# A gated convolution with expert routing: where the second part's routing and the first part's scatters stand

## Chip, cores, metric

The kernel runs on one core of a Trainium2 chip. The metric is the device time of one execution in microseconds (us), as the median of several. All data is float32. The core's engines are TensorE (PE; its weight loads are shown as PEld), VectorE (DVE), ScalarE (ACT), GpSimd (POOL) and SyncE (SP), which here only issues transfers. Each engine runs its instructions in the order of the program and waits on semaphores for the others.

## What is computed

Eight sequences of 3584 tokens with 192 channels pass a causal convolution with 7 softmax-weighted taps per head, and then a layer of 8 experts in which a token may take over the expert of the token before it.

```python
# lightweight convolution: w = softmax(weight) over the 7 taps of each of 8 heads
out[b, s, h] = sum_k w[h, k] * x_pad[b, s + k, h]          # then x = out

logits     = x @ w_gate                                    # (B, S, 8)
local_gate = sigmoid(x @ w_local)
for b in range(B):
    prev_e = -1
    for s in range(S):
        fresh_e = argmax(logits[b, s])
        e = fresh_e if s == 0 or local_gate[b, s] < 0.5 else prev_e
        prev_e = e
        p = softmax(logits[b, s])
        h = maximum(x[b, s] @ w1[e], 0)                    # 192 -> 1024
        out[b, s] = p[e] * (h @ w2[e])                     # 1024 -> 192
```

## The kernel before

The 28672 tokens are worked through in 16 parts of 1792 tokens. For each part the kernel convolves, routes (which expert, which slot among that expert's tokens) and scatters the rows to `slots` in memory, sorted by expert, by indirect transfers of GpSimd. Blocks of 128 tokens (the first 35) and then of 256 tokens of one expert each are loaded from there, multiplied with that expert's weights, and their results are scattered to the output. Tables say which block is which expert's. Blocks 0 to 6 need rows of part 0 only, 7 to 13 rows of part 0 and the first half of part 1, 14 to 20 parts 0 and 1.

Parts 0 and 1 are convolved on TensorE (`wide`) and routed by `wide_route`. Blocks 0 and 1 do not wait for the scatters: their rows are picked by matrix products with one-hot matrices (`hots`, `gather`, `gathered`).

```python
def wide_route(g, y_sb, lt):                  # a generator; the caller takes it on stage by stage
    ...                                       # VectorE: fr, fc, mx, ex
    yield                                     # 1
    ...                                       # VectorE: eq, key
    nc.scalar.activation(ex, ex, Act.Exp)     # L419
    ...                                       # VectorE: fc (L420)
    yield                                     # 2
    ...                                       # TensorE: two transposes of fc (L426)
    yield                                     # 3
    mark["nf", g] = nc.vector.tensor_copy(nf, rps[:, 1, :])
    ...                                       # VectorE: scans; run (L452)
    nc.tensor.transpose(bps, run, identity=ident[:NB, :NB])          # L454
    ...
    yield                                     # 4
    mark["oh", g] = nc.vector.tensor_tensor(oh, bcast_mid(bps, E), bcast(en[:TB], NB),
                                            op=Alu.is_equal)
    ...                                       # TensorE: counts of oh (L468, L469)
    yield                                     # 5
    mark["upto", g] = nc.vector.tensor_tensor_scan(...)
    ...                                       # VectorE: slots of the tokens
    for b in range(NB):                       # 16 scatters stand ready
        to_put.append((HALF if g and b < NH else g, y[:, b, :], posi[:, b:b + 1]))
    yield                                     # 6
    if g == 0:
        first_table(upto[:, :, NB], pos)      # which has hots(0) in its middle
    ...
    if g:
        for _ in tables(g):                   # small VectorE instructions
            pass

def hots(i):                                  # 4 VectorE instructions (L550)
    ...
def gather(i, y_sb, ps, blocks):
    for b in blocks:
        nc.tensor.matmul(ps[:, :Y0 + D], lhsT=hot[:TB, i, b, :], rhs=y_sb[:TB, b, :Y0 + D],
                         start=(b == 0), stop=(b == NB - 1))         # L556
def gathered(ps):
    xg = xp.tile([P, KT, DG], F32, name="xg")
    nc.scalar.copy(xg[:, 0, :Y0 + D], ps[:, :Y0 + D])                # L561
    ...
    return xg
```

`put` sends one scatter from GpSimd, behind another instruction if one is named. The convolution of part 2 and later parts is done by VectorE and ScalarE (`conv`), and `step(t)` takes it, or a later part's routing, on by about t us of VectorE's time.

```python
def conv(g, x_sb):
    ...
    def first(h):                             # ScalarE (L378)
        nc.scalar.activation(cols(h), chans(h, 0), Act.Copy, scale=c[:, h, 0:1])
    first(0)
    yield 0
    for h in range(H):
        if h + 1 < H:
            first(h + 1)
        ...
        for k in range(1, KC):                # VectorE (L388)
            nc.vector.scalar_tensor_tensor(cols(h), chans(h, k), c[:, h, k:k + 1],
                                           cols(h), Alu.mult, Alu.add)
            yield 0.6
```

A block is `turn` (its rows transposed on TensorE), `hidden` (first product, relu on ScalarE) and `output` (second product). `output` writes the two `yps` buffers, which ScalarE and then VectorE read. The start of the block phase:

```python
puts_behind(None, 5)                          # 5 scatters of part 0
rest(route0)                                  # the first table
some(wide1, WIDE - 20)
...
weights(AHEAD - 1)                            # weights of three blocks
picks = [yps_p.tile([P, 512], F32, name="yps")]
gather(0, ya, picks[0], range(4))
rest(wide1)
puts_behind(mark["lt", 1], 3)
route1 = wide_route(1, yb, got.pop(1))
some(route1, 2)
hots(1)
gather(0, ya, picks[0], range(4, NB))
next(route1)
xgs[0] = gathered(picks[0])
...                                           # gather(1), turn of block 0, gathered(1) among
...                                           # the stages of route1 and two steps (1.8, 2.4)
puts_behind(mark["upto", 1], 4)
rest(route1)
for i, (_, n, _, _) in enumerate(blocks):
    ensure(i)                                 # row loads up to three blocks ahead
    weights(i + AHEAD)
    ...
    hT = hidden(n, wbs[i], xT, (1, 1) if i else (0, 0))     # (1, 1): scatters behind its relus
    if i + 1 < len(blocks):
        xT, copied = turn(blocks[i + 1][1], xgs[i + 1])
        ...
    step(2.1 if n == 1 else 4.2)
    output(n, wbs.pop(i), xgs.pop(i), hT)                   # has a step(1.2) inside
    step(1.3 if n == 1 else 3.0)
```

Of the kernel before, what the change touches and what calls it, by code (L numbers as in the profile page):

```python
# [17 lines left out]
P = 128  # L18
# [11 lines left out]
NB = 16  # L30
# [40 lines left out]
def bcast(ap, n):  # L71

    return ap.rearrange("p (a o) -> p a o", o=1).to_broadcast([ap.shape[0], ap.shape[1], n])


def bcast_mid(ap, n):

    return ap.rearrange("p (o a) -> p o a", o=1).to_broadcast([ap.shape[0], n, ap.shape[1]])
# [3 lines left out]
def kernel(  # L82
# [100 lines left out]
        nc.vector.tensor_copy(c.rearrange("p h k -> p (h k)"), cps[:, H:H + H * KC])  # L183
    wgb, wgq = wg[:, :3, :], wg[:, 3:, :]

    got, mark = {}, {}

# [5 lines left out]
    def wide(g, xv, y_sb, both):  # L195

        lps = yps_p.tile([P, 512], F32, name="yps")[:, :4 * TB].rearrange("p (q s) -> p q s", s=TB)  # L200
        count = [0]

        def mine():
            count[0] += 1
            return both and count[0] % 2 == 0

        def convolve(half, heads):
            bs = slice(half * NH, (half + 1) * NH)
            for h in heads:
                ps = hps_p.tile([P, 512], F32, name="hps")[:TB, :NH * GS]  # L210
                nc.tensor.matmul(ps, lhsT=hank[:NI, h, :],
                                 rhs=xv[:NI, bs, h * GS:(h + 1) * GS], start=True, stop=True)
                to = y_sb[:TB, bs, Y0 + h * GS:Y0 + (h + 1) * GS]
                at = ps.rearrange("p (b d) -> p b d", d=GS)
                if mine():
                    nc.vector.tensor_scalar(to, at, rz[:TB, h:h + 1], None, Alu.mult)
                else:
                    nc.scalar.activation(to, at, Act.Copy, scale=rz[:TB, h:h + 1])
                yield

        def again(half):
            bs = slice(half * NH, (half + 1) * NH)
            nc.gpsimd.tensor_copy(yr[:, bs, :], y_sb[:TB, bs, Y0 + P:Y0 + D])
            nc.gpsimd.tensor_copy(y_sb[:TB, bs, Y0 + D:IX], y_sb[:TB, bs, Y0:Y0 + DR])

        def turned(half, qs):
            at = half * 3 * NH // 2
            for q in qs:
                tps = hps_p.tile([P, 512], F32, name="hps")[:, :4 * TB].rearrange(
                    "p (u s) -> p u s", s=TB)  # L230
                for u in range(4):
                    b = half * NH + (q * 4 + u if q < 2 else 2 * u)
                    src = (y_sb[:TB, b, Y0:Y0 + P] if q < 2
                           else yr[:, b:b + 2, :].rearrange("p b d -> p (b d)"))
                    nc.tensor.transpose(tps[:, u, :], src, identity=ident[:TB, :TB])
                leave = nc.vector.tensor_copy if mine() else nc.scalar.copy
                leave(yT[:, at + 4 * q:at + 4 * q + 4, :], tps)
                yield

        def products():  # L240
            for j in range(4):
                u = j // 2 * 3 * NH // 2 + j % 2 * 4
                nc.tensor.matmul(lps[Q * j:Q * j + Q], lhsT=wgb[:, 0, :], rhs=yT[:, u:u + 4, :],
                                 start=True, stop=False, skip_group_check=True)
            for i in range(2):
                for j in range(4):
                    u = j // 2 * 3 * NH // 2 + NH + j % 2 * 2
                    nc.tensor.matmul(lps[Q * j:Q * j + Q, i::2, :], lhsT=wgb[:, 1 + i, :],
                                     rhs=yT[:, u:u + 2, :], start=False, stop=(i == 1),
                                     skip_group_check=True)  # L250

        yield from convolve(0, range(H))
        zy = z_tile()
        yT = zy[:, :3 * NH * TB].rearrange("p (u s) -> p u s", s=TB)
        yr = zy[:TB, 3 * NH * TB:].rearrange("p (b d) -> p b d", d=DR)
        again(0)
        yield from convolve(1, range(5))
        yield from turned(0, (0, 1))
        yield from convolve(1, range(5, H))
        yield from turned(0, (2,))  # L260
        again(1)
        yield from turned(1, range(3))
        products()
        if both:
            nc.vector.tensor_copy(lsb[:, :2, :], lps[:, :2, :])
            nc.scalar.copy(lsb[:, 2:, :], lps[:, 2:, :])
        else:
            nc.scalar.copy(lsb, lps)
        yield
        ltp = yps_p.tile([P, 512], F32, name="yps")[:TB].rearrange("p (q c) -> p q c", c=P)  # L270
        for q in range(4):
            nc.tensor.transpose(ltp[:, q, :], lsb[:, q, :], identity=ident)
        lt = sm.tile([P, NB, E + 1], F32, name="lt")[:TB]
        mark["lt", g] = nc.vector.tensor_copy(lt.rearrange("p (j q) e -> p j q e", q=4),
                              ltp.rearrange("p q (j c) -> p j q c", c=Q)[:, :, :, :E + 1])
        got[g] = lt

# [116 lines left out]
    def wide_route(g, y_sb, lt):  # L394
# [41 lines left out]
        yield  # L436
        run = sm.tile([NB, TB], F32, name="run")
        nf = sm.tile([NB, TB], F32, name="nf")
        mark["nf", g] = nc.vector.tensor_copy(nf, rps[:, 1, :])
        nc.vector.tensor_tensor_scan(run, nf, rps[:, 0, :], 0.0, Alu.mult, Alu.add)  # L440

        nc.vector.tensor_reduce(rows[:NB, 1, 0:1], nf, axis=AX.X, op=Alu.min)
# [17 lines left out]
        if g:  # L460
            norm()
        yield
        oh = sm.tile([P, E, NB], F32, name="oh", bufs=1)[:TB]
        mark["oh", g] = nc.vector.tensor_tensor(oh, bcast_mid(bps, E), bcast(en[:TB], NB),
                                                op=Alu.is_equal)


# [5 lines left out]
        nc.vector.tensor_reduce(pr, eq, axis=AX.X, op=Alu.add)  # L473
        yield
        upto = sm.tile([P, E, 1 + NB], F32, name="upto")
        mark["upto", g] = nc.vector.tensor_tensor_scan(upto.rearrange("p e b -> p (e b)"),
                                     go_on.rearrange("p e b -> p (e b)"),
                                     nps[:, :E * (1 + NB)], 0.0, Alu.mult, Alu.add)
        at = sm.tile([P, E, NB], F32, name="at", bufs=1)[:TB]
# [23 lines left out]
    def first_table(upto, pos):  # L503
# [24 lines left out]
        nc.vector.scalar_tensor_tensor(rel, bcast(r2[:TB], NB), -float(UT), bcast_mid(pos, 2),  # L528
                                       Alu.mult, Alu.add)
        rels.append(rel)  # L530
        hots(0)

        inn = sm.tile([P, E], F32, name="inn")
        nc.vector.tensor_scalar(inn, end[:, :E], i_of, None, Alu.is_le)
# [12 lines left out]
    def hots(i):  # L547
        for b in range(0, NB, NB // 4):
            bs = slice(b, b + NB // 4)
            nc.vector.tensor_tensor(hot[:TB, i, bs, :], bcast(rels[0][:, i, bs], UT),  # L550
                                    bcast_mid(slot[:TB], NB // 4), op=Alu.is_equal)
# [218 lines left out]
    def put(behind=None):  # L770


        if not to_put:
            return
        g, rows, to = to_put.pop(0)
        nc.gpsimd.nop()
        ins = nc.gpsimd.indirect_dma_start(  # L777
            out=slots[:, :], in_=rows, in_offset=None,
            out_offset=bass.IndirectOffsetOnAxis(ap=to, axis=0)).ins
        if behind is not None:  # L780
            tc.add_manual_dep(ins, behind.ins.name, SYNC, reason="scatters apart")
        if puts:
            tc.declare_no_dep(ins, group="puts", reason="slots of their own")
        if g:
            tc.declare_no_dep(ins, group="gets", reason="those slots were full before")
        puts.append((g, ins))
        tc.add_to_no_dep_group("puts", ins)
        tc.add_to_no_dep_group(f"puts{g}", ins)
# [285 lines left out]
    for n in (4, 3, 5, 1, 3, 0):  # L1074
        next(route0)
        some(wide1, n)

    def puts_behind(ins, n):
        for _ in range(n):
            put(ins)  # L1080

    puts_behind(None, 5)
    rest(route0)
    some(wide1, WIDE - 20)

# [23 lines left out]
    weights(AHEAD - 1)  # L1109


    picks = [yps_p.tile([P, 512], F32, name="yps")]
    gather(0, ya, picks[0], range(4))
    rest(wide1)
    puts_behind(mark["lt", 1], 3)
    route1 = wide_route(1, yb, got.pop(1))
    some(route1, 2)
    hots(1)
    gather(0, ya, picks[0], range(4, NB))
    next(route1)  # L1120
    xgs[0] = gathered(picks[0])
    picks.append(yps_p.tile([P, 512], F32, name="yps"))
    gather(1, ya, picks[1], range(9))
    next(route1)
    puts_behind(mark["nf", 1], 2)
    step(1.8)
    xT, _ = turn(blocks[0][1], xgs[0])
    gather(1, ya, picks[1], range(9, NB))
    next(route1)
    puts_behind(mark["oh", 1], 2)  # L1130
    step(2.4)
    xgs[1] = gathered(picks[1])
    next(route1)
    puts_behind(mark["upto", 1], 4)
    rest(route1)
    for i, (_, n, _, _) in enumerate(blocks):
        st["block"] = i
        ensure(i)
        weights(i + AHEAD)
        if i == LATE:  # L1140
            x_in[3] = load_x(3)
        hT = hidden(n, wbs[i], xT, (1, 1) if i else (0, 0))
        if i + 1 < len(blocks):
            xT, copied = turn(blocks[i + 1][1], xgs[i + 1])
            if len(to_put) > NT // 2 and n == KT:
                put(copied)
        step(2.1 if n == 1 else 4.2)
        output(n, wbs.pop(i), xgs.pop(i), hT)
        step(1.3 if n == 1 else 3.0)

    kind, _, at, group = spare[0]
# [78 lines left out]
```

## Time and profile before

| | us |
|---|---|
| time, median of 3 | 1355.3 (1355.29 to 1356.96) |
| span of the profiled execution | 1351.2 |
| TensorE busy | 1327.7 |
| VectorE busy | 780.0 |
| ScalarE busy | 512.1 |
| GpSimd busy | 492.6 |

A line of the timeline gives the start in us from the span's start, the duration in us, the engine, the kernel's line, the operation with the tiles it writes and reads and their sizes, how many instructions are merged into the line, and in brackets how long the engine stood idle before it and what ended the wait. A line of the windows gives, for a stretch of time, its length, the busy time of each engine with the count of instructions in the order PE, PEld, DVE, ACT, POOL, and at the end the share of the TensorE clock that was granted, the busy share of the DMA engines, and GB/s. A line of the waits gives who waited for whom, the sum in us, the number of times, and the longest. Starts of matmuls are recorded; their ends are modelled.

### The profile page before, as it was taken

To read this page: it belongs to the slowest core of one execution; us is meant where nothing else is said; L and a number is where in the kernel's file an instruction comes from. 1 tells how busy PE (TensorE), PEld (TensorE's weight loads), DVE (VectorE), ACT (ScalarE), POOL (GpSimd) and SP (SyncE) were. 2 spreads that over 40 slices of the span, in tenths; PEclk is the share of its full clock that TensorE was granted. 3 is DMA by queue.
4 is the path that set the end of the run, shared out by engine and by line. 5 is a ranking of instruction groups with operands and counts; after the bars stand their busy time and mean duration, and the time that the engine had idled before them with its cause. 6 is when DMAs were issued, how large, how long until landed. Compare 5 with 4: busy or idle time off the path is not lost. (4 is left out here: it accounts for less than half of the span.)

```text
span 1351.2 us, 41902 instructions
## 1 busy us (share of the span) xinstructions
PE 1327.7 (98%) x17140; PEld 1298.5 (96%) x17140; DVE 780.0 (58%) x2434; ACT 512.1 (38%) x1147; POOL 492.6 (36%) x538
## 2 busy tenths in 40 slices
PE   8899999999999999999999999999999999999998
PEld 7799999999999999999999999999999999999997
DVE  6878887886868787868787878786610000000000
ACT  5244443433343433333334343433333333333333
POOL 4455343534243434343434343434344211221111
PEclk9899999999999999999999999999999999999999
DMA  5899999967575757575757575756566555556993
GB/s 185 291 343 402 365 364 337 389 245 268 199 272 195 289 195 291 198 273 203 280 202 287 196 287 198 289 203 228 199 232 228 199 183 182 190 189 232 322 325 124
DMA packets 67299, 340.39 MB, mean 252 GB/s; under 512 B 12576, under 2 KB 23191, under 8 KB 47650
## 3 DMA queue, kind: packets, MB, share of 16 engines
q1 hardware_dynamic: 44784, 284.88, 58.7%
q0 software_dynamic: 22320, 52.82, 10.3%
q8 instruction: 136, 2.23, 0.6%
q14 instruction: 57, 0.47, 0.1%
q10 hardware_dynamic: 2, 0.00, 0.0%
HBM read 284.73 MB, written 53.41 MB: 250 GB/s over the span
## 5 line engine op out<-in xcount | busy, mean ns | idle before, releaser
L977 PE MATMUL yps<-wb,hT 64*128 64x192 f32 x7328 | 652.9, 326 | 9.6 <-ACT hT L965 7.7
L960 PE MATMUL hps<-xT,wb 64*128 64x256 f32 (+1 forms) x6816 | 640.2, 337 | 0.6 <-issue 0.6
L977 PEld LDWEIGHTS yps<-wb,hT 64*128 64x128 f32 x7328 | 609.7, 188 | 21.0 <-ACT hT L965 14.0
L960 PEld LDWEIGHTS hps<-xT,wb 64*128 64x128 f32 x6816 | 610.0, 188 | 8.4 <-issue 1.8
L993 POOL DMA_INDIRECT out_dram<-o_sb,xg x229 | 232.4, 1015 | 613.7 <-DVE o_sb L989 545.9
L965 ACT ACTIVATE hT<-hps 128x512 f32<-128x512 f32 (+1 forms) x568 | 262.3, 512 | 407.5 <-PE hps L960 306.8
L388 DVE SCALAR_TENSOR_TENSOR y_sb<-x_sb,c,y_sb 128x336 f32<-128x336 f32 x672 | 377.0, 571 | 19.5 <-ACT y_sb L378 1.4
L989 DVE SCALAR_TENSOR_TENSOR o_sb<-yps,xg,o_sb 128x192 f32<-128x192 f32 x229 | 87.4, 413 | 489.1 <-ACT o_sb L985 474.5
L777 POOL DMA_INDIRECT slots<-y_sb,posi x228 | 227.7, 999 | 216.0 <-ACT hT L965 112.0
L985 ACT ACTIVATE o_sb<-yps,xg 128x192 f32<-128x192 f32 x229 | 86.9, 418 | 379.1 <-PE yps L977 368.7
L946 ACT COPY xT<-xps 128x768 f32<-128x768 f32 (+1 forms) x142 | 96.7, 681 | 5.3 <-issue 1.6
L360 PEld LDWEIGHTS xps<-ident,xg 64*128 64x128 f32 x1374 | 81.9, 139 | 2.7
L360 PE MATMUL xps<-ident,xg 64*128 64x64 f32 x1374 | 80.4, 222 | 0.0
L378 ACT ACTIVATE y_sb<-x_sb,c 128x336 f32<-128x336 f32 x112 | 64.6, 589 | 0.0
L572 DVE STREAM_TRANSPOSE z<-y_sb 128x768 f32<-128x768 f32 (+1 forms) x56 | 45.4, 852 | 0.4
L598 DVE COPY lt<-lq 32x36 f32<-32x36 f32 x224 | 41.0, 183 | 3.5
L582 PE MATMUL hps<-z,wg 64*32 64x128 f32 x1344 | 24.1, 272 | 0.7 <-issue 0.6
L582 PEld LDWEIGHTS hps<-z,wg 64*32 64x32 f32 x1344 | 19.1, 105 | 3.4 <-issue 2.6
L556 PE MATMUL yps<-y_sb 112*128 112x194 f32 x64 | 12.5, 351 | 1.8 <-DVE y_sb L550 1.6
L556 PEld LDWEIGHTS yps<-y_sb 112*128 112x128 f32 x64 | 11.2, 201 | 2.6 <-DVE y_sb L550 2.0
L590 DVE STREAM_TRANSPOSE lq<-ls 128x256 f32<-128x256 f32 x14 | 6.2, 444 | 12.4 <-ACT ls L587 12.4
L568 POOL COPY y_sb<-y_sb 128x896 f32<-128x896 f32 x14 | 13.4, 954 | 0.0
(239 smaller groups left out, 374.4 us busy)
## 6 DMA issues: line engine op xcount, KB each, us to landing
wb<-in_w_dram SPq DMA_DIRECT2D x138, 1536.0 KB
x_sb<-in_x_dram SPq DMA_DIRECT2D x14, 1920.0 KB
xg<-slots SPq DMA_DIRECT2D x87, 259.0 KB
xg<-slots SPq DMA_DIRECT2D x53, 129.5 KB
wb<-in_w_dram SPq DMA_DIRECT2D x12, 512.0 KB
out_dram<-o_sb,xg POOLq DMA_INDIRECT x229
slots<-y_sb,posi POOLq DMA_INDIRECT x228
x_sb<-in_xb_dram SPq DMA_DIRECT2D x4, 768.0 KB
```

The lines of the kernel that those rows point to most:

```text
L360: nc.tensor.transpose(to, src[rows], identity=ident[rows, rows])
L378: nc.scalar.activation(cols(h), chans(h, 0), Act.Copy, scale=c[:, h, 0:1])
L388: nc.vector.scalar_tensor_tensor(cols(h), chans(h, k), c[:, h, k:k + 1], cols(h), Alu.mult, Alu.add)
L572: nc.vector.transpose(z[:, t:u, :], y_sb[:, t:u, Y0:Y0 + D])
L777: ins = nc.gpsimd.indirect_dma_start(out=slots[:, :], in_=rows, in_offset=None, out_offset=bass.IndirectOffsetOnAxis(ap=to, axis=0)).ins
L946: copied = nc.scalar.copy(to, at)
L960: nc.tensor.matmul(hps[half][:, j, w], lhsT=wb[rows, f0:f0 + P], rhs=xT[rows, d, w], start=(d == 0 and j == 0), stop=(d == KD - 1), skip_g ...
L965: relu = nc.scalar.activation(hT[:, m:m + 2, w], hps[half][:, :, w], Act.Relu)
L977: nc.tensor.matmul(yps[half][:, k * D:(k + 1) * D], lhsT=hT[rows, m, k * P:(k + 1) * P], rhs=wb[rows, WA + m * D:WA + (m + 1) * D], start= ...
L985: nc.scalar.activation(o_sb[:, k, :], y[k][0], Act.Copy, scale=xg[:, k, 0:1])
L989: nc.vector.scalar_tensor_tensor(o_sb[:, k, :], y[k][1], xg[:, k, 0:1], o_sb[:, k, :], Alu.mult, Alu.add)
L993: sent = nc.gpsimd.indirect_dma_start(out=out, in_=o_sb[:, k, :], in_offset=None, out_offset=bass.IndirectOffsetOnAxis(ap=xg.bitcast(I32)[ ...
```

## The change

Part 0's 16 scatters, which stood in groups of 5, 3, 2, 2 and 4 behind marked VectorE instructions, are issued in one row. The one-hot matrices of block 0 are made after the first table and no longer in its middle. Both gathers are done in one loop with nothing of part 1's routing in it, and the step of the convolution follows them in one piece. The routing of part 1 is then spread: two stages ahead of the blocks, one in block 0, two in block 1, and the rest ahead of block 2; since its scatters are ready later, blocks 2 and 3 send three each and not two. Fewer waits are tied to marked instructions this way, and block 0 no longer has the whole routing of part 1 ahead of it. The results are the same.

```diff
@@ first_table
         rels.append(rel)
-        hots(0)
 
         inn = sm.tile([P, E], F32, name="inn")
@@ before the blocks
-    puts_behind(None, 5)
+    while to_put:
+        put()
     rest(route0)
     some(wide1, WIDE - 20)
...
-    picks = [yps_p.tile([P, 512], F32, name="yps")]
-    gather(0, ya, picks[0], range(4))
+    for i in range(2):
+        hots(i)
+        pick = yps_p.tile([P, 512], F32, name="yps")
+        gather(i, ya, pick, range(NB // 2))
+        if i:
+            xT, _ = turn(blocks[0][1], xgs[0])
+        gather(i, ya, pick, range(NB // 2, NB))
+        xgs[i] = gathered(pick)
+    step(5.4)
     rest(wide1)
-    puts_behind(mark["lt", 1], 3)
     route1 = wide_route(1, yb, got.pop(1))
     some(route1, 2)
-    hots(1)
-    gather(0, ya, picks[0], range(4, NB))
-    next(route1)
-    xgs[0] = gathered(picks[0])
-    picks.append(yps_p.tile([P, 512], F32, name="yps"))
-    gather(1, ya, picks[1], range(9))
-    next(route1)
-    puts_behind(mark["nf", 1], 2)
-    step(1.8)
-    xT, _ = turn(blocks[0][1], xgs[0])
-    gather(1, ya, picks[1], range(9, NB))
-    next(route1)
-    puts_behind(mark["oh", 1], 2)
-    step(2.4)
-    xgs[1] = gathered(picks[1])
-    next(route1)
-    puts_behind(mark["upto", 1], 4)
-    rest(route1)
@@ the blocks
-        hT = hidden(n, wbs[i], xT, (1, 1) if i else (0, 0))
+        if i == 2:
+            rest(route1)
+        hT = hidden(n, wbs[i], xT, {0: (0, 0), 2: (1, 2), 3: (1, 2)}.get(i, (1, 1)))
         if i + 1 < len(blocks):
             xT, copied = turn(blocks[i + 1][1], xgs[i + 1])
             if len(to_put) > NT // 2 and n == KT:
                 put(copied)
+        if i < 2:
+            next(route1)
         step(2.1 if n == 1 else 4.2)
         output(n, wbs.pop(i), xgs.pop(i), hT)
+        if i == 1:
+            next(route1)
         step(1.3 if n == 1 else 3.0)
```

More of the change, by code (lines that the diff above doesn't have):

```diff
@@ L184 @@
     wgb, wgq = wg[:, :3, :], wg[:, 3:, :]
-    got, mark = {}, {}
+    got = {}
     def z_tile():
@@ L273, in wide @@
         lt = sm.tile([P, NB, E + 1], F32, name="lt")[:TB]
-        mark["lt", g] = nc.vector.tensor_copy(lt.rearrange("p (j q) e -> p j q e", q=4),
+        nc.vector.tensor_copy(lt.rearrange("p (j q) e -> p j q e", q=4),
                               ltp.rearrange("p q (j c) -> p j q c", c=Q)[:, :, :, :E + 1])
@@ L438, in wide_route @@
         nf = sm.tile([NB, TB], F32, name="nf")
-        mark["nf", g] = nc.vector.tensor_copy(nf, rps[:, 1, :])
+        nc.vector.tensor_copy(nf, rps[:, 1, :])
         nc.vector.tensor_tensor_scan(run, nf, rps[:, 0, :], 0.0, Alu.mult, Alu.add)
@@ L463, in wide_route @@
         oh = sm.tile([P, E, NB], F32, name="oh", bufs=1)[:TB]
-        mark["oh", g] = nc.vector.tensor_tensor(oh, bcast_mid(bps, E), bcast(en[:TB], NB),
+        nc.vector.tensor_tensor(oh, bcast_mid(bps, E), bcast(en[:TB], NB),
                                                 op=Alu.is_equal)
@@ L475, in wide_route @@
         upto = sm.tile([P, E, 1 + NB], F32, name="upto")
-        mark["upto", g] = nc.vector.tensor_tensor_scan(upto.rearrange("p e b -> p (e b)"),
+        nc.vector.tensor_tensor_scan(upto.rearrange("p e b -> p (e b)"),
                                      go_on.rearrange("p e b -> p (e b)"),
@@ L1076 @@
         some(wide1, n)
-    def puts_behind(ins, n):
-        for _ in range(n):
-            put(ins)
-    puts_behind(None, 5)
+    while to_put:
+        put()
     rest(route0)
```

## The prediction

> **What bounds the kernel now.** I read the page's busy shares first, then the waits of TensorE and of VectorE in stretches, then the first 90 us of the timeline.
>
> ```profile
> PE 1327.7 (98%) x17140; PEld 1298.5 (96%) x17140; DVE 780.0 (58%) x2434; ACT 512.1 (38%) x1147; POOL 492.6 (36%) x538
> PE   8899999999999999999999999999999999999998
> DVE  6878887886868787868787878786610000000000
> ```
>
> TensorE is busy for 98% of the span. From 58 us to the end it waits little; the largest of its waits there:
>
> ```profile
> PE yps L977 <- ACT hT L965: 4.8, 15, 0.7
> ```
>
> So whatever delays TensorE before about 90 us is paid in full at the end: afterwards there is no idle time that could absorb it. The change touches only the time from 28 us on to the first blocks, so the question is when TensorE gets through block 4 or so. The timeline there:
>
> ```profile
> 30.02 2.59 DVE L550 TENSOR_TENSOR y_sb<-rel,wb 112x512 f32<-112x512 f32 x4
> 35.93 0.31 ACT L419 ACTIVATE ex<-ex 112x128 f32<-112x128 f32 x1 [4.70 <-DVE eq L416]
> 36.25 0.22 DVE L420 SCALAR_TENSOR_TENSOR fc<-key,fr 112x16 f32<-112x16 f32 x1
> ...
> 40.24 0.32 ACT L561 COPY xg<-yps 128x194 f32<-128x194 f32 x1 [3.99 <-PE yps L556]
> 40.61 1.07 ACT L378 ACTIVATE y_sb<-x_sb,c 128x336 f32<-128x336 f32 x2
> 42.51 0.22 PE L454 MATMUL hps<-ident,run 16*112 16x16 f32 x1 [2.09 <-DVE run L452]
> ...
> 55.43 2.93 PE L977 MATMUL yps<-wb,hT 64*128 64x192 f32 x16 [2.91 <-ACT hT L965]
> ...
> 57.67 0.17 DVE L852 SCALAR_TENSOR_TENSOR used<-new,used 128x8 f32<-128x8 f32 x1
> ```
>
> Every engine works in program order, and ScalarE's order is the one to watch: the convolution's first taps (L378) stand behind the copy of a gathered block (L561), and the exponential of the routing (L419) waits for VectorE. VectorE has finished the whole second routing (L852) at 57.8 us, under block 0. After that, between 58 and 84 us, it is nearly as tight as TensorE. This is all it waits there:
>
> ```profile
> DVE o_sb L989 <- ACT o_sb L985: 0.9, 2, 0.5
> ```
>
> One block of 128 tokens costs VectorE nine taps (0.57 us each, L388) and one L989 (0.42), 5.6 us; it costs TensorE about 2.85 + 2.82 = 5.7 us. A delay of VectorE in this stretch cannot be made up. Two windows show the price of an idle TensorE:
>
> ```profile
> 52.00:54.00 2.00, 0.52 (x7) 0.23 (x3) 1.73 (x12) 0.00 (x0) 1.60 (x2) 1.00 0.37 109
> 56.00:58.00 2.00, 2.00 (x16) 2.00 (x14) 1.76 (x12) 0.03 (x1) 0.00 (x0) 0.50 0.38 88
> 58.00:60.00 2.00, 2.00 (x22) 2.00 (x20) 1.90 (x4) 0.89 (x2) 0.00 (x0) 0.50 0.80 198
> ```
>
> After the gap of 2.9 us the granted clock (third number from the right) is 0.50.
>
> **What the Trainium skill says.** "TensorE: Matmul & The Clock Gate", "Architectural detail": ScalarE and VectorE are strict FIFOs. The trace agrees (L419 held ScalarE for 4.70 us). The same page, "Part 1: The HAM clock gate": a mostly idle window of about 3.4 us halves the clock, and a busy one gives it back. The trace agrees (0.50 after the 2.9 us gap, for nearly 7 us). "DMA: Bandwidth & Descriptors", "Anatomy of one DMA": a GpSimd transfer carries some 2 us of completion. Here the last of the 16 scatters starts at 52.96 us and the sync engine issues the first row load at 55.75.
>
> **The change, part by part.**
>
> *Scatters.* They start at 28.55 in both. In a row they follow at 1.25 us (31.28, 32.52, 33.77), after a first step of 1.48: the last starts at 28.55 + 1.48 + 14 x 1.245 = 47.5 instead of 52.96. The row loads for blocks 2 and 3, and the fourth weights behind them on the same queue, leave at about 50 instead of 55.75. TensorE needs block 2's rows only behind block 1, at 62.5 now, so this gains nothing by itself.
>
> *Table before one-hots.* The first four one-hots (2.5 us) move behind the table, whose entries are then ready at about 31.2 instead of 33.75. Weights start 2.5 us earlier. Block 0 did not visibly wait for them (its start at 47.59 stands behind the gather).
>
> *Gathers.* Now VectorE: table done 31.5, hots(0) to 34.0, hots(1) to 36.5. TensorE: gather(0) from 32.3, 16 x 0.345 us (4.11 us for 12 blocks) = 5.5, to 37.9; half of gather(1) to 40.6, the turn of block 0 to 41.0, the other half to 43.8. The copy of block 1 on ScalarE ends at 44.6. Block 0's first product can start at about 44.5, 3 us earlier than 47.59.
>
> *The convolution behind the gather.* Here I see the loss. The call of 5.4 us (ten taps) now stands after both gathers, so its first ScalarE taps come after the copy of block 1. VectorE, done with hots(1) at 36.5, idles until about 45.2: **8.7 us**. In the kernel before it used that time for the routing.
>
> *The routing behind the convolution.* Ten taps take until 51.0. From lt to fc the routing takes 2.45 us (34.02 to 36.47 now), so fc comes at 53.5. The exponential (L419) stands in ScalarE ahead of block 0's relu, so relu starts at about 53.3. TensorE has finished block 0's first product at 47.4 and idles to 53.5, **6 us**, then runs output(0) at half clock, to about 59.5. That is still about level with the kernel before (58.3).
>
> *Routing steps among the blocks.* Block 0 costs VectorE six more taps and L989 (waiting for output(0), 60.0), then three taps, and the scan part 2.17 us (40.28 to 42.45): run at 63.9. TensorE waits some 1.5 us for it. Then 0.8 of normalization, six taps and L989 (68.6), and the one-hot at 68.9: TensorE waits another 1.8 us. Block 2 starts at 69.7 where it now starts at 65.3. Then the rest of the routing, 9.2 us (48.51 to 57.76), falls on VectorE in one piece: 69.6 + 1.7 (three taps) + 9.2 = 80.5. Six taps of block 2 make it 84.0, L989 of block 2 84.4. TensorE can't start output(3) before that, since the two output buffers (yps) must both be free; it now starts it at 75.0. **Lag: 84.5 - 75.0 = 9.5 us.** TensorE would have been ready at 79.6, so it idles 4.9 us and its clock may drop once more: 0 to 3 us on top. Later routing steps and transfers follow TensorE's pace and shift with it.
>
> *Sum.* +9.5 as lag, +1 to 2 for the clock, minus about 1 as I have rounded waits upward: **+10 us**, 1365.
>
> **Rivals.** (a) *The earlier rows and weights win.* If the stall at 52.5 to 55.4 came from transfers, an earlier start would remove it, and with block 0 starting 3 us earlier the kernel would end at some 1350. For it: around it the chip moves only 58 to 109 GB/s, so something is late. Against it: the weights were issued by 43 us, and rows are not needed until block 2; and the stall does not sit in the VectorE chain that I count. (b) *The lag is absorbed.* VectorE is busy 58% over the span, so a lag of routing might be swallowed: +2 to +4 us, 1358. For it: VectorE idles in the last third. Against it: the hold is use of the output buffers in block 3, up to where VectorE has 0.9 us of slack. (c) *Worse:* repeated half-clock stretches in blocks 1 to 4, each costing 1.7 to 3.4 us, and signals from TensorE that reach ScalarE late (3.99 us at 40.24 though the gather's matmuls had been issued by 36.8), which would push the copy of block 1, and all behind it, by 1 to 4 us: 1372. For it: both occur in the kernel before. Against: a shorter wait need not cross the idle limit.
>
> **Range and chances.** Between (b) and (c) lie 1357 to 1373; (a) has some 10%. 2% are 27 us, beyond anything in a stretch of 60 us that I can name; so within 2% is 0.96, slower 0.03, faster 0.01.
>
> **What would show it.** VectorE idle from about 36.5 to 45 with ScalarE's L378 behind the second L561; the exponential L419 at about 53 and relu of block 0 behind it; TensorE gaps of about 6 us ahead of L426, 1 to 2 us at L454 and L468, and 3 to 6 us ahead of output(3), named after VectorE's L989; half clock after them; and no more gaps later. I am wrong if VectorE works through 36 to 45, or if TensorE's block 5 begins no later than now.

## The result, and the profile after

| | before | after | ratio, 95% interval |
|---|---|---|---|
| time, us, median of 4 | 1355.3 | 1388.1 | 1.0233 [1.0203, 1.0262] |
| span of the profiled execution, us | 1351.2 | 1387.7 | |
| TensorE busy, us | 1327.7 | 1341.1 | |

The change costs 32.8 us where +10 was predicted. The busy shares and slices of the kernel after:

```profile
PE 1341.1 (97%) x17140; PEld 1291.4 (93%) x17140; DVE 784.1 (57%) x2434; ACT 511.0 (37%) x1147; POOL 489.1 (35%) x538
PE   8579999999999999999999999999999999999998
DVE  6387888877787877777777778676610000000000
```

The same 17140 matmuls are recorded, and they are busy 13.4 us longer. The group that grew most is that of the logits (L582 before, L581 after):

```profile
L582 PE MATMUL hps<-z,wg 64*32 64x128 f32 x1344 | 24.1, 272 | 0.7 <-issue 0.6
L581 PE MATMUL hps<-z,wg 64*32 64x128 f32 x1344 | 30.7, 273 | 5.3 <-issue 5.0
```

(Here come the time in which any of the group was busy, the mean of one in ns, and the idle time ahead of them with its main cause.) One logits matmul takes as long as before, but they follow each other less closely: 6.6 us more of busy and 4.6 us more of idle time. The gathers' matmuls did run at half clock in part, 410 ns each where they took 351. In the second and third slice (35 to 104 us) TensorE is down to 0.5 and 0.7, where it was at 0.8 and 0.9 before. But not all of the loss is there: by the time of the same VectorE instruction of each block, the kernel after is 10.0 us late in block 0, 12.3 in block 1, 21.7 in block 2, 26.1 in block 34 (the last of 128 tokens), and 36.5 at the end. Something goes on costing time behind the stretch that the prediction covers. The waits of TensorE from 104 us on (who waited for whom, sum in us, times, longest):

```profile
PE yps L976 <- ACT hT L964: 5.3, 18, 0.7
PE hps L581 <- issue: 5.0, 19, 0.4
```

The first is the old wait for relu (4.8 us before). The second is new at this size: TensorE stalls, without a cause that the trace names, in the logits matmuls (L581) of later parts. Now the early stretch, 30 to 130 us, TensorE's waits and VectorE's and ScalarE's longest (those two up to 90 us):

```profile
PE xps L360 <- ACT xg L560: 9.7, 1, 9.7
PE hps L426 <- ACT hT L964: 5.8, 1, 5.8
PE yps L976 <- DVE o_sb L988: 3.6, 1, 3.6
...
PE hps L468 <- DVE oh L464: 1.2, 1, 1.2
...
PE hps L454 <- DVE run L452: 1.0, 1, 1.0
...
DVE y_sb L388 <- ACT y_sb L378: 22.1, 1, 22.1
...
ACT xg L560 <- remote: 20.8, 1, 20.8
```

Four of TensorE's waits are the predicted ones: L426, output(3) behind L988, L468, L454. The first, 9.7 us, is not among them. ScalarE sat for 20.8 us before the copy of block 0's gathered rows (L560), and "remote" means that a signal ended the wait, but that nothing which could have sent it had ended just before. The timeline around it, one line per engine and event:

```profile
35.71 5.26 PE L555 MATMUL yps<-y_sb 112*128 112x194 f32 x31
...
46.51 0.94 POOL L776 DMA_INDIRECT slots<-y_sb,posi  x1 [0.30 <-issue]
...
50.27 0.32 ACT L560 COPY xg<-yps 128x194 f32<-128x194 f32 x1 [20.77 <-remote]
...
50.64 0.58 PE L360 MATMUL xps<-ident,xg 64*128 64x64 f32 x6 [9.67 <-ACT xg L560]
...
56.41 0.32 ACT L560 COPY xg<-yps 128x194 f32<-128x194 f32 x1 [4.66 <-PE yps L555]
...
56.74 1.50 PE L959 MATMUL hps<-xT,wb 64*128 64x128 f32 x22
56.78 1.54 ACT L378 ACTIVATE y_sb<-x_sb,c 128x336 f32<-128x336 f32 x3
```

The last matmul of gather(0) started at 38.0 us, and 16 more started behind it up to 40.7. The copy that needs it ran at **50.27**, 2.8 us after the last of the 16 scatters had left GpSimd (46.51 + 0.94). The trace's record of semaphores has TensorE's update at 50.25. So the update itself was late, and not ScalarE; whether the matmul was held or only its signal, the trace can't tell, since ends of matmuls are modelled. I call it a late signal. Only then did the turn of block 0 follow, and block 0's first product began at 56.74 us. And the granted clock (third number from the right) in windows there and near output(3):

```profile
44.00:48.00 4.00, 0.00 (x0) 0.00 (x0) 0.00 (x0) 0.00 (x0) 2.82 (x3) 0.71 1.02 400
48.00:50.00 2.00, 0.00 (x0) 0.00 (x0) 0.00 (x0) 0.00 (x0) 0.00 (x0) 0.50 0.36 129
...
54.00:56.00 2.00, 2.00 (x8) 2.00 (x7) 0.00 (x0) 0.00 (x0) 0.00 (x0) 0.52 0.00 0
56.00:58.00 2.00, 2.00 (x29) 1.80 (x29) 0.57 (x1) 1.59 (x6) 0.00 (x0) 1.00 0.08 12
...
96.00:98.00 2.00, 2.00 (x16) 2.00 (x14) 1.89 (x5) 0.00 (x0) 1.39 (x3) 0.50 1.01 430
```

Between 44 and 50 us no engine but GpSimd has any work recorded, and the second gather, up to 56 us, then runs at half clock.

### The profile page after: what moved, and what is told of

It is laid out like the page before. It is cut to its first block, busy times and chain, and to the rows that moved or that the text cites. A ratio compares the mean times of both kernels' runs of the same rounds, so it can differ in the third digit from the quotient of the medians.

```text
span 1387.7 us, 41896 instructions
## 1 busy us (share of the span) xinstructions
PE 1341.1 (97%) x17140; PEld 1291.4 (93%) x17140; DVE 784.1 (57%) x2434; ACT 511.0 (37%) x1147; POOL 489.1 (35%) x538
## 3 DMA queue, kind: packets, MB, share of 16 engines
q0 software_dynamic: 22320, 52.82, 10.1%
## 5 line engine op out<-in xcount | busy, mean ns | idle before, releaser
L959 PE MATMUL hps<-xT,wb 64*128 64x256 f32 (+1 forms) x6816 | 641.0, 337 | 2.6 <-issue 1.4
L976 PEld LDWEIGHTS yps<-wb,hT 64*128 64x128 f32 x7328 | 608.5, 188 | 17.7 <-ACT hT L964 11.7
L959 PEld LDWEIGHTS hps<-xT,wb 64*128 64x128 f32 x6816 | 594.8, 188 | 26.7 <-issue 8.0
L388 DVE SCALAR_TENSOR_TENSOR y_sb<-x_sb,c,y_sb 128x336 f32<-128x336 f32 x672 | 383.1, 582 | 71.6 <-issue 30.2
L988 DVE SCALAR_TENSOR_TENSOR o_sb<-yps,xg,o_sb 128x192 f32<-128x192 f32 x229 | 87.1, 412 | 442.8 <-ACT o_sb L984 424.7
L360 PEld LDWEIGHTS xps<-ident,xg 64*128 64x128 f32 x1374 | 77.7, 139 | 13.8 <-ACT xg L560 10.0
L360 PE MATMUL xps<-ident,xg 64*128 64x64 f32 x1374 | 77.2, 222 | 9.7 <-ACT xg L560 9.7
L378 ACT ACTIVATE y_sb<-x_sb,c 128x336 f32<-128x336 f32 x112 | 63.4, 591 | 0.0
L597 DVE COPY lt<-lq 32x36 f32<-32x36 f32 x224 | 40.7, 182 | 3.4
L581 PE MATMUL hps<-z,wg 64*32 64x128 f32 x1344 | 30.7, 273 | 5.3 <-issue 5.0
L581 PEld LDWEIGHTS hps<-z,wg 64*32 64x32 f32 x1344 | 21.1, 105 | 13.6 <-issue 10.9
L586 ACT COPY ls<-hps 128x128 f32<-128x128 f32 x28 | 6.1, 269 | 40.3 <-remote 27.4
L555 PEld LDWEIGHTS yps<-y_sb 112*128 112x128 f32 x64 | 14.5, 248 | 3.5 <-DVE y_sb L549 3.3
```

What stands on the lines that cost most here:

```text
L360: nc.tensor.transpose(to, src[rows], identity=ident[rows, rows])
L581: nc.tensor.matmul(lps[half][Q * j:Q * j + Q, :], lhsT=wgq[rows, b, :], rhs=z[rows, begin[j]:begin[j] + TQ, b * Q:(b + 1) * Q], start=(b = ...
L959: nc.tensor.matmul(hps[half][:, j, w], lhsT=wb[rows, f0:f0 + P], rhs=xT[rows, d, w], start=(d == 0 and j == 0), stop=(d == KD - 1), skip_g ...
L976: nc.tensor.matmul(yps[half][:, k * D:(k + 1) * D], lhsT=hT[rows, m, k * P:(k + 1) * P], rhs=wb[rows, WA + m * D:WA + (m + 1) * D], start= ...
L988: nc.vector.scalar_tensor_tensor(o_sb[:, k, :], y[k][1], xg[:, k, 0:1], o_sb[:, k, :], Alu.mult, Alu.add)
```

## The experiments

Three theories came out of this. **Chain**: the predicted one, VectorE's and ScalarE's order around the convolution and routing, worth some 10 us. **Row**: while 16 scatters leave GpSimd without a break, TensorE's signals do not reach ScalarE, so block 0 starts 12 us late; this is independent of the order of the routing. **Tap shift**: the change lets ten taps of part 2 pass ahead of the blocks instead of eight (a step of 5.4 for steps of 1.8 and 2.4), which moves every later part's stages by two taps. In TensorE's order the logits matmuls of part 4 and of parts 6 to 15 stand between a block's turn and its output in the kernel before, and behind an output in the kernel after (those of parts 2, 3 and 5 move the other way), and would lose a little in each part. The expectations below call Row theory A, Chain theory B and Tap shift theory C; D, E and W are rivals that are told there.

The runs were on four chips, numbered 0, 1, 7 and 14, and each is compared with the kernel before on its own chip. That matters here: the kernel before takes 1354 to 1355 us on chips 0 and 7, and 1332.6 to 1332.9 on 14 and 1. I call the first kind late-signal and the second prompt-signal chips, for a reason that the runs give. The chip of the recorded pair is not on record; by its time (1355.3) and its late copy it is of the first kind.

### Chip 14: one part at a time

The row alone, in the kernel before:

```diff
-    puts_behind(None, 5)
+    puts_behind(None, 16)
 ...                       # the other four puts_behind are left out
```

> The kernel before with all 16 scatters of part 0 in one row and nothing else changed. Theory A (a row of GpSimd scatters holds back TensorE's signals to ScalarE and VectorE until the row ends): the copy of gathered block 0 waits until about 50 us, not 40.2, and the time rises by 8 to 12 us, to 1363 to 1367. Theory B (all the loss is the VectorE chain of the spread routing and its later parts): the copy stays near 40, the time stays within 2 us of 1355.

Measured: 1333.3 against 1332.6 us, ratio 1.0003 [0.9994, 1.0012].

The row broken up, in the kernel after (5 scatters, 4 more behind the copy of block 0's rows, 7 behind that of block 1's):

```diff
-    while to_put:
+    for _ in range(5):
         put()
 ...
-        xgs[i] = gathered(pick)
+        xgs[i], done = gathered(pick)   # done: the last copy in it
+        for _ in range((4, 7)[i]):
+            put(done)
```

> The changed kernel with its 16 scatters in groups of 5, 4 and 7, the second behind the copy of gathered block 0 and the third behind that of block 1. Theory A: the copy of block 0 starts at 38 to 40 us, not 50.3, and the time falls by 9 to 12 us, to 1376 to 1379. Theory B: no change, 1386 to 1390, since VectorE's chain is as before.

Measured: 1346.6 us, 1.0103 [1.0086, 1.0120].

Eight taps in the kernel after:

```diff
-    step(5.4)
+    step(4.7)
```

> The changed kernel with 8 convolution taps and not 10 ahead of block 0. In program order this puts the logits products of parts 7 to 16 back between the two products of a block, where the kernel before has them, instead of behind both. Theory C (those two taps shift all later stages against the blocks, and cost about 1.2 us for each later part): the time falls by 11 to 13 us, to 1375 to 1377, and the lag behind the kernel before no longer grows after block 10. Theory D (the growth is a backlog of scatters left by the late start): a fall by the two taps alone, 1 to 2 us.

Measured: 1344.1 us, 1.0087 [1.0070, 1.0104].

Ten taps in the kernel before:

```diff
-    step(2.4)
+    step(3.5)
```

> The kernel before with 10 taps and not 8 ahead of block 0. Theory C: later parts take the changed kernel's order, the time rises by 11 to 14 us, to 1366 to 1369, about evenly over the run. Theory D: up by 1 to 2 us, at the start alone.

Measured: 1335.1 us, 1.0019 [1.0012, 1.0026].

By these, the row costs nothing and the tap shift 2.5 us. Row and tap shift would be dead, and with them most of the loss. But the kernel after itself was not measured on chip 14, and that chip runs the kernel before nearly 23 us faster than it ran when the change was measured. So the question became whether the change costs 33 us there at all.

### Chip 7: the change itself, and the convolution ahead of the gathers

> The kernel before itself, for its trace on the chip of this call. Theory A: TensorE's signal for the gather of block 0 comes at about 40 us, and that for the second half of block 0's first product at about 55. Theory B has nothing to say of it; if both come within 0.5 us of the matmul, the hold is a matter of the chip and not of the kernel alone.

> The changed kernel itself, on the chip of this call. In the first comparison it took 32.8 us more than the kernel before, with TensorE's signal for the gather of block 0 about 12 us late. Theory B (VectorE's chain alone, all signals prompt): 10 to 15 us over the kernel before, with the copy of block 0 at about 37 us. Theory A (a row of scatters always holds the signals): 30 us or more, the copy at about 50 us.

Measured: before 1356.0 in a single run beside 1354.2 for its other runs; after 1385.7 us, 1.0236 [1.0219, 1.0253]. The recorded result is repeated here: +31.5.

```diff
+    hots(0)
+    hots(1)
+    step(5.4)
     for i in range(2):
-        hots(i)
         ...
-    step(5.4)
```

> The changed kernel with both one-hots and the ten taps moved ahead of both gathers, so that the taps no longer stand behind the copies of blocks 0 and 1 in ScalarE's order and VectorE works through the gather. Theory B: VectorE's idle time of 8 us or more before the taps goes, TensorE's gap of some 6 us ahead of the transposes of fc goes with it, and the time falls by 6 to 9 us against the changed kernel on the same chip. Theory E (the lump of routing ahead of block 2 and the output buffers set the loss): a fall of 0 to 2 us.

Measured: 1378.9 us, 1.0187 [1.0168, 1.0207], 6.8 us less than after. ScalarE's three taps now run at 29.7 us, ahead of the copies, so VectorE no longer waits for them, and TensorE's wait ahead of L426 is gone. Yet the copy of block 0's rows still ran only at 49.27, having waited 18.0 us for a "remote" signal, and VectorE stood 13.3 us at L274 behind TensorE instead. Mending this part of the chain gains 6.8 of 31.5 us; most of the loss is still there.

### Chip 1: the same kernels again

So far there are two explanations: kernels differ, or chips do.

> The changed kernel itself. On a chip like 14, where no signal is late: 12 to 15 us over the kernel before, which is theory B's chain of VectorE alone, with block 0's first product at about 44 us. On a chip like 7: 31 us over it, as before.

Measured: 1346.5 us, 1.0097 [1.0075, 1.0120]: **13.6 us** over the kernel before on this chip, not 31.5. The chip makes the difference. Its timeline of ScalarE, with block 0's first product on TensorE (L959), shows what the kernel after looks like when the signals come:

```profile
38.28 0.32 ACT L560 COPY xg<-yps 128x194 f32<-128x194 f32 x1 [9.51 <-PE yps L555]
...
44.40 2.95 PE L959 MATMUL hps<-xT,wb 64*128 64x128 f32 x48
44.44 1.53 ACT L378 ACTIVATE y_sb<-x_sb,c 128x336 f32<-128x336 f32 x3
52.72 0.31 ACT L419 ACTIVATE ex<-ex 112x128 f32<-112x128 f32 x1 [6.74 <-DVE eq L416]
```

The copy is at 38.28 (predicted 37.9) and not at 50.27, although 16 scatters leave GpSimd in the same row, the last at 46.40. Its waits of TensorE, and VectorE's longest:

```profile
PE hps L426 <- ACT hT L964: 5.8, 1, 5.8
PE yps L976 <- DVE o_sb L988: 4.6, 1, 4.6
...
DVE y_sb L388 <- ACT y_sb L378: 9.8, 1, 9.8
```

This is the predicted picture, nearly number by number.

> The kernel before with all 16 scatters in one row, a second time, since two chips have been met: chip 14, where TensorE's signals came at once and the kernel before took 1332.6 us, and chip 7, where they came late and it took 1354.2. On a chip like 7, theory A: TensorE's signal for the gather of block 0 comes when the row ends, at about 49 us and not at 40.8; up by 6 to 12 us. Theory W (the weight transfers and not the scatters hold the signals): at about 41, no change. On a chip like 14: no change, as before.

> The changed kernel with its scatters in groups of 5, 4 and 7, again. On a chip like 7, theory A: the copy of block 0 starts at 38 to 40 us and not at 47 to 50, block 0's first product at 45 to 47 and not 54.5 to 57, and the time falls by 9 to 12 us against the changed kernel. Theory W: the copy stays at 47 or later, since the same weights are under way. On a chip like 14: 1346, as before.

> The kernel before with 10 taps and not 8, again. On a chip like 7, theory C: up by 6 to 13 us, spread over the later parts, as the lag of the changed kernel grows there from 20 to 27 or from 22 to 36 us. Theory D: up by 1 to 2 us. On a chip like 14: 1335, as before.

Measured: 1333.1, 1346.9 and 1335.4 us against 1332.9; ratios 1.0003 [0.9993, 1.0014], 1.0102 [1.0080, 1.0124] and 1.0017 [1.0010, 1.0024]. They repeat chip 14. Breaking the row up in after changes nothing here (1346.9 and 1346.5).

### Chip 0: the same three on a late-signal chip

> The kernel before with all 16 scatters in one row. So far only seen on chips where TensorE's signals come at once (there no change). On a chip like 7, theory A: the signal for the gather of block 0 comes at about 49 us and not at 40.8; up by 6 to 12 us. Theory W (weight transfers hold the signals, not scatters): about 41, within 2 us. On a chip like 14 or 1: no change.

Measured: 1365.7 against 1355.0 us, 1.0080 [1.0064, 1.0097], **+10.7** for the row alone. ScalarE's, VectorE's and TensorE's timeline:

```profile
50.51 0.32 ACT L561 COPY xg<-yps 128x194 f32<-128x194 f32 x1 [14.99 <-remote]
...
50.55 0.26 DVE L439 COPY nf<-hps 16x112 f32<-16x112 f32 x1 [12.38 <-remote]
...
52.79 0.27 PE L454 MATMUL hps<-ident,run 16*112 16x16 f32 x1 [13.07 <-DVE run L452]
```

With the routing in its old place, the copy again waits until 50.51, behind the row's end (46.83 + 0.94), and TensorE stands for 13.07 us. VectorE waited for another of TensorE's signals (the transposes of L426, which ran at 35.9), and it went on 0.04 us after ScalarE. So it is TensorE's signals that are held, and they come together; VectorE's own signal passed during the row (TensorE took up L556 at 36.52 after 0.27 us of waiting for L550). Nor is every signal of TensorE held: by the record of semaphores, that of L272 came at 32.1, under the fourth scatter, without delay. In the same kernel on chip 1 the copy is at 36.45.

> The changed kernel with its scatters in groups of 5, 4 and 7. So far only seen on chips with prompt signals (there as the changed kernel). On a chip like 7, theory A: the copy of block 0 starts at 38 to 41 us and not at 47 to 50, and the time falls by 9 to 12 us against the changed kernel, to some 20 us over the kernel before. Theory W: the copy stays at 47 or later, 31 us over.

Measured: 1374.5 us, 1.0152 [1.0135, 1.0169]: +19.5, 12 less than after on chip 7. The two copies in it:

```profile
36.92 0.32 ACT L560 COPY xg<-yps 128x194 f32<-128x194 f32 x1 [7.23 <-PE yps L555]
...
42.72 0.32 ACT L560 COPY xg<-yps 128x194 f32<-128x194 f32 x1 [2.35 <-PE yps L555]
```

They come as early as on a prompt-signal chip. The weights (the expectation's theory W) are not what holds the signals: from 36 to 44 us, when both copies run, the DMA engines' busy share is 1.02 here. So it is the unbroken row: 11 us of cost put in alone, 12 us gained when taken out. The groups don't remove all lateness. The last seven scatters, up to 51.9 us, still hold a signal of block 0's first product (a relu at 53.59, 1.38 us for "remote"); it costs little there, because ScalarE stands behind the exponential until 51.36 in any case.

> The kernel before with 10 taps and not 8. Where signals are prompt it cost 2.5 us. On a chip like 7, theory C (the shifted order of the later parts is dear there): up by 6 to 13 us, spread over the later parts. Theory D: up by 2 to 3 us as elsewhere.

Measured: 1365.6 us, 1.0082 [1.0065, 1.0099], **+10.6** for two taps, against +2.5 on prompt-signal chips. The groups of the logits matmuls and of the copy behind them:

```profile
L582 PE MATMUL hps<-z,wg 64*32 64x128 f32 x1344 | 29.8, 273 | 4.4 <-issue 4.2
...
L587 ACT COPY ls<-hps 128x128 f32<-128x128 f32 x28 | 6.1, 269 | 40.2 <-remote 30.9
```

In the kernel before on chip 7, the first of these lines, and then what the copy waited for:

```profile
L582 PE MATMUL hps<-z,wg 64*32 64x128 f32 x1344 | 26.3, 272 | 1.8 <-issue 1.7
```

```profile
  PE hps L582: 17.3, 14
```

With eight taps the copy waits 17.3 us in 14 times for its matmuls and never for "remote"; with ten it waits 30.9 us for "remote" in nine times and 9.3 for its matmuls. These are TensorE's late signals again: in nine of the 14 parts two scatters now leave back to back about the end of the logits (at 340.3 and 341.6 us, for one; in the kernel before they are 2.8 us apart there), and the copy comes 2.0 to 2.6 us after the last matmul, where it came at most 1.2 us after. The price shows in TensorE's own line: the logits' busy and idle time grew by 6.1 us, and this trace, of the fastest of the four runs, is 6.6 us longer than that of the kernel before on chip 7.

On the same chip I tried for a kernel that beats both, aiming at the old wait for relu: both of a block's scatters go behind its second relu, where each relu had one.

```diff
-        hT = hidden(n, wbs[i], xT, (1, 1) if i else (0, 0))
+        hT = hidden(n, wbs[i], xT, (0, 2) if i else (0, 0))
```

> The kernel before with both scatters of a block behind its second pair of relus, none behind the first. On a chip like 7, theory A: the second pair then waits no longer for a late signal, TensorE's short gaps ahead of the second half of a block's second product go in the first 35 blocks, and the time falls by 3 to 15 us, as such gaps are part of the 22 us by which that chip is slower. Where signals are prompt: within 1 us of the kernel before.

Measured: 1369.8 us, 1.0111 [1.0094, 1.0127]: a miss. The group of the logits:

```profile
L582 PE MATMUL hps<-z,wg 64*32 64x128 f32 x1344 | 38.9, 274 | 11.7 <-issue 10.9
```

L977's idle time fell from the 9.1 us that it has in the kernel before on chip 7 to 3.7 us (matmuls of output), but the logits stalled for 11.7 us and took 38.9 instead of 26.3. The scatters went out in pairs, with the logits in their old places in TensorE's order. So the place in the order is not the whole condition; it is how scatters and logits meet.

### Chip 7 again: both repairs together

After with the three groups of a_groups and the eight taps of a_8taps.

> After with both repairs at once: the scatters in three groups (5, then 4 behind the copy of block 0's rows, then 7 behind the copy of block 1's) and 8 taps instead of 10 ahead of the blocks. If the loss on chips with late signals is the sum of three terms, row (some 12 us), tap shift (some 10) and the predicted chain of VectorE and ScalarE (some 10), only the chain is left: 9 to 13 us over before on such a chip. If row and tap shift were one cause seen twice, taking both away would bring no more than either alone: 20 us over before. On a chip with prompt signals both theories say 10 to 12 us over before.

Measured: 1366.8 against 1353.6 us, 1.0088 [1.0066, 1.0111]: +13.2. TensorE's two longest waits of the chain, from 30 to 130 us:

```profile
PE yps L976 <- DVE o_sb L988: 3.5, 1, 3.5
...
PE hps L426 <- ACT hT L964: 2.7, 1, 2.7
```

The waits ahead of L468 and L454 are the chain's too (1.2 and 1.0 us); the logits are back at an idle time of 2.6 us. The chain is left, with little else: ScalarE still waits twice for "remote" up to 90 us (3.7 and 2.7 us), so that 13.2 is not the chain alone. By the time of each block this trace is 10.1 us behind the kernel before at block 2, 9.9 at block 20 and 11.2 at the end.

And the placing of b_relu2 for the blocks of 128 tokens only (n is 1). The expectation calls the pair of numbers VectorE's share; it is the count of scatters behind the first and the second relu.

```diff
-        hT = hidden(n, wbs[i], xT, (1, 1) if i else (0, 0))
+        hT = hidden(n, wbs[i], xT, ((0, 2) if n == 1 else (1, 1)) if i else (0, 0))
```

> Before with both relu tiles on VectorE's share changed for the blocks of one part only ((0, 2) instead of (1, 1) when n is 1; block 0 and the longer blocks as they are). The early wide run in which the same was done for all blocks was ahead by 1 to 7 us up to about block 45 and lost later. If what it gained belongs to the relu waits of short blocks, this is 3 to 7 us faster than before on a late-signal chip and within 1 us on a prompt one; if any change of the shares moves the logits matmuls of later parts next to scatters, it is slower by 5 us or more on a late-signal chip.

Measured: 1353.6 against 1353.6 us, 0.9998 [0.9990, 1.0005]. Neither expectation held: no gain and no loss. From 120 us on, TensorE's wait for relu fell from the 3.6 us of the kernel before to 0.2, and its stall in the logits rose from 1.7 to 3.8 us. No version that I ran beats the kernel before.

## Why the prediction was wrong

The direction and the chain were right, the size was not: 32.8 us instead of 10. In three terms, as they measured by undoing them in turn on chips 7, 0 and 7, each against the kernel before on that chip: after is 31.5 us over before; without the row 19.5; without row and tap shift 13.2. So the **row** is 12 us, the **tap shift** 6 (10.6 when put into the kernel before alone, so between 6 and 11 by what stands around it), and what is left, the **chain**, 13.2 with an interval of 8.9 to 15. The chain is thus what the prediction had at +10; it was not taken out as a whole in any run. On prompt-signal chips: row 0, tap shift 2.1 (13.6 less the 11.5 of a_8taps, on two chips) to 2.5, chain 11.5.

*Scatters.* The pace was right: the last started at 46.51 us (47.5 predicted, from a row that began 1 us later). That the row "gains nothing by itself" was right in its way, too: no earlier row load made anything faster. That it costs something, I did not consider.

*Gathers: the step that failed.* I let the gathers go "to 37.9" and then the copies, and had block 0's first product at 44.5. The matmuls were on time (38.0), but the copy that they release ran at 50.27, and the first product came at 56.74, 12 us later than predicted. The assumption under the step is that a matmul's signal arrives when the matmul ends. On chip 1 it did, and the first product is at 44.40. On the late-signal chips it did not, once some scatters of an unbroken group had left, until the group was over. The kernel before shows the sign twice:

```profile
37.51 0.99 POOL L777 DMA_INDIRECT slots<-y_sb,posi  x1 [0.30 <-issue]
...
55.00 0.66 ACT L965 ACTIVATE hT<-hps 128x256 f32<-128x256 f32 x2 [4.92 <-remote]
```

The first eight scatters leave it without a break, the eighth until 38.50, and the copy at 40.24, with 3.99 us of idle time ahead of it, came 1.7 us behind that. The relu at 55.00 came 1.1 us behind the last of all scatters (52.96 + 0.94). I put the first into rival (c), as a delay of "1 to 4 us", and did not see that the length of the unbroken group set it. The row of 16 has no break, and so the delay lasted to its end.

*The convolution behind the gather.* Right: VectorE idle for 8.7 us predicted, 9.8 on chip 1, with L378 behind the second copy (44.44; 44.6 for the copy's end predicted). In the recorded pair it was 22.1 us, the same wait stretched by the row.

*The routing behind the convolution.* Right: the exponential at 52.72 on chip 1 (about 53), TensorE's gap ahead of L426 5.8 us (6). The gap has that length in the recorded pair too, since the whole chain is only displaced by the row.

*Routing steps among the blocks.* Right in order, a little too large in each: L454 1.0 in the recorded pair (1.5), L468 1.2 (1.8), output(3) 3.6 in the recorded pair and 4.6 on chip 1 (4.9). VectorE's last instruction of block 2 was predicted at 84.4 and came at 83.3 on chip 1. The lag of "9.5 us" was 10.1 at block 2 in a_groups8.

*What was left out.* "No more gaps later" was wrong. The two taps more ahead of the blocks were counted as VectorE's time only. That they shift where each later part's logits stand is not in the prediction at all. The lag that grows behind block 34 goes with it: from 26.1 to 36.5 us in the kernel after, but from 9.9 to 11.2 in a_groups8.

*Rivals and range.* (a) and (b) fell. The stall at 52.5 to 55.4, for which (a) suspected transfers, ended with the relu at 55.00, a late signal. (c) named the late signal and had a third of its size. The low weight on "slower" came from the sentence that 2% are "beyond anything in a stretch of 60 us that I can name"; a wait tied to the length of a row of 16 transfers was not among those named.

**What stays open.** Why chips 0 and 7 hold TensorE's signals and 1 and 14 don't, no run shows; that they do so during scatters is shown, but by what path is not, nor how many scatters it takes. In the tap shift, the displaced logits are shown to go with the loss and the late signals. Pairs of scatters beside the logits go with it in b_10taps and in b_relu2 on chip 0, but which neighbourhood of scatter and matmul is the harmful one is not settled.

## What to carry to other kernels

On some chips a long, unbroken row of indirect transfers from GpSimd costs time on engines that have nothing to do with it (10.7 us for 16 on chip 0, nothing on 1 and 14). Where a short wait of ScalarE for TensorE is seen beside scatters, count it for as long as the row will last, and leave breaks, or put the row where nobody waits for TensorE. A change in how much background work goes ahead of a loop can move all of that work against the loop's other work, to the end of the kernel, as two taps did here; look where it lands. And measure a change and its undoing on the same chip: the same kernels gave 13.6 and 31.5 us here.

## What was not expected of the hardware

- The same program takes 1332.6 to 1332.9 us on two chips and 1354 to 1355 on two others, 1.7%. By the trace of b_row16 on chip 1 (as fast there as the kernel before), the kernel before on chip 7 is 2.8 us behind at block 0, 18.7 at block 34 and 25.2 at the end.
- On the slower kind of chip a matmul's signal came 12 us late (recorded pair) and 14 us late (b_row16 on chip 0) while 16 scatters (0.94 us each, 1.25 us apart) were leaving GpSimd, some 2.7 us after the last had left.
- In the kernel after, TensorE was busy again from 50.64 us, but the clock was still 0.52 in the window from 54 to 56 us and full from 56 on, some 5.3 us later. The Trainium skill ("TensorE: Matmul & The Clock Gate", "Part 1: The HAM clock gate") has a busy window of some 3.4 us giving it back, in windows that run on by themselves. 5.3 us, between one and two windows, fits, if the window has to be busy from its start.
